# A hand-ordered list of operations replaced by another: sliding attention and a token-mixing MLP on one core

## The chip, the cores and the metric

The kernel runs on one core of one Trainium2 chip. The metric is the device time of one execution in microseconds (us); of several runs the median is given. A profile is one further execution, recorded by the hardware profiler; its span goes from the first to the last instruction that the profiler sees.

A core has five engines that work side by side, each through its own instructions in the order in which they were issued: TensorE (PE in the profile; its weight loads are the row PEld), VectorE (DVE), ScalarE (ACT), GpSimd (POOL) and SyncE (SP), which here only starts DMA transfers. They wait for one another through semaphores. All inputs and outputs are bfloat16.

## The reference

The input `x` is [1, 2048, 512]: 2048 tokens of 512 numbers. Six modulation rows come from a condition `c`. The first part is an attention in which each token looks at itself and at seven earlier tokens, two apart; the second is an MLP that mixes tokens.

```python
mod = (silu(c) @ w_mod).reshape(c.shape[0], 6, 1, -1)
sa, ca, ga, sb, cb, gb = mod[:, 0], ..., mod[:, 5]
h = layernorm(x) * (1 + ca) + sa
# attention: 32 heads of 16; token s attends to s, s-2, ..., s-14
q, k, v = split(h @ wqkv)
logits = einsum('bhsd,bhswd->bhsw', q, k[idx]) * 16 ** -0.5   # masked where idx < 0
o = einsum('bhsw,bhswd->bhsd', softmax(logits), v[idx])
x = x + ga * (o @ wo)
h = layernorm(x) * (1 + cb) + sb
# MLP over tokens: w1 is [2048, 1792], w2 is [1792, 2048]
h = layernorm(h)
u = gelu(einsum('bsd,sf->bdf', h, w1) + b1)
y = einsum('bdf,fs->bds', u, w2) + b2
return x + gb * transpose(y)
```

## The kernel before

**Tiling.** The tokens are 16 tiles of 128. The attention runs over five chunks of 2, 4, 4, 4 and 2 tiles (`SIZES`, chunks 0 to 4). The MLP needs all tokens for each of its 14 output tiles; it is cut into sweeps over the tiles that are ready, and partial sums are parked.

**How the order is made.** The kernel body adds operations to a graph (`_Graph.add`), each with a name, an engine, what it reads and writes, and the buffers that it takes and frees. The text `ORDER` (L182) lists 762 tokens: 760 names and two fillers. `_Graph.schedule` goes through it from front to back and checks that all that an operation depends on stands ahead of it. The loop behind `order = G.schedule()` (L1005) then issues them one by one. Each engine receives its own instructions in the order of this list, and SyncE its DMA starts. So the list decides, for each engine, what stands behind what; a waiting instruction holds up all that stand behind it on its engine, and nothing on the others. A token can carry a mark: `:a`, `:d`, `:p` puts an operation that has a choice on ScalarE, VectorE or GpSimd. `:q` makes `mm()` write each 128-column matmul as four matmuls of 32 columns, each with its own weight load, one behind the other at `tile_position=(0, j)`. `fill:K:N` issues N matmuls of 128x128 on the identity into PSUM buffer `psS[K]`; nobody reads them.

**Buffers.** There are six PSUM buffers `psS` of 512 columns and a double one, `psL`, for logits; a ring of four buffers `big` of 1 MB, and a ring of five, `vd` (tile `vD`). A buffer is given to an operation when the list reaches it: the one freed longest ago in the list. So a new order also gives out other buffers, and the wait for a buffer is a wait for its last reader.

**Recording.** All instructions are issued from one helper (`_EngProxy.wrapped`), so the profile shows L133 for all of them; they are told apart by tiles and shapes.

**Stages and names.** In a name the first number is the chunk, or for single tiles the tile.

- Start: `ident` and `consts` make constants on GpSimd; `ld_c`, `ld_x*`, `ld_wmod*`, `ld_wqkv*` load. `cps`, `silu_exp`, `silu_dve` make silu(c); `modcols1` and `a1col` make the column 1+ca. `wsc{t}_{kt}` multiplies one 128x512 block of the raw Q, K or V weights (t = 0, 1, 2) by it, into `w_qkv`. `ln1s`, `rstd1`, `nb1`, `n1` are the first LayerNorm, `tr` and `hT` (chunks 0, 1) or `xt` (DMA, later chunks) its transpose. `warm` issues nine idle matmuls.
- Attention: `qkv{chunk}_{t}{j}` are the projections and `ev` copies them out of PSUM. `qk{chunk}_{dlo}` multiplies q with the eight shifted k on VectorE, 128x4096 numbers in a chunk of four tiles; `red` sums the products over four of the 16 numbers of a head by matmuls with a 0/1 matrix (`group4`), always as four 32-column tiles. `max`, `sub`, `exp`, `esum`, `rcp`, `smB` are the softmax: VectorE, TensorE, ScalarE, TensorE, ScalarE, VectorE. `a2` and `vd` are DMAs that spread the weights and v over partitions; `halo` copies the 16 tokens ahead of a chunk. `pv` multiplies (VectorE, 128x4096 again), `pvacc` sums (TensorE, four tiles), `oev` copies out.
- Behind it, by tile: `wo` is the output projection, with x added by an identity matmul; `x1` copies it out, `ln2q`, `ln2m`, `rstd2`, `nb2`, `n2` are the second LayerNorm, `aff` the modulation, `ln3s`, `rstd3`, `nb3`, `h3` the third. `modcol`, `mcols`, `mrowt`, `mrows` make the modulation rows, and `st_row`, `ld_row` send them through DRAM to be spread over the partitions as `rows_bc` (0: ga, needed by `woq_s`; 1: sb, 1+cb and gb, needed by `aff`).
- MLP: `mlp1_{sweep}_{ft}_{tile}` are the first layer's matmuls for output tile `ft` from that token tile on; `park` copies partial sums to `gT`, `inj` brings them back, `padd` adds them, `gelu` ends the layer. `mlp2`, `fin` and `st_out` are the second layer, its scaling and the stores.

Of the kernel before, what the change touches and what calls it, by code (L numbers as in the profile page):

```python
# [41 lines left out]
class _Graph:  # L42
# [42 lines left out]
    def schedule(self):  # L85
        by_name = {o.name: o for o in self.ops}
        held = {p: [None] * n for p, n in self.pools.items()}
        freed = {p: [-1] * n for p, n in self.pools.items()}
        done, order = set(), []
        for pos, token in enumerate(ORDER.split()):  # L90
            name, *rest = token.split(":")
            if name == "fill":
                k, n = map(int, rest)
                f = _Op(-1, [("pe", 0.06 * n, lambda k=k, n=n: self.fill_fn(k, n))], 0.0, "filler", 0)
                f.alloc = f.frees = f.behind = None
                order.append(f)
                continue
# [6 lines left out]
            if o.alloc is not None:  # L104
                p = o.alloc.pool
# [82 lines left out]
hT1_3:a qkv0_00 sab ev0_12:d n1_6 ld_wmod4 qvb0 ln1s14 ld_wo1 qkv0_02 qvb_cp0 ln1s15 ev0_00:a wsc2_2 qvb1  # L188
wsc2_0:d qkv1_00 wsc2_3 ev0_10:a ev0_02:d ln1s10 wsc2_1:d qkv1_10 qvb_cp1 qk0_0 ev1_10:a qkv0_22 qk0_1 n1_7
qkv0_20 ln1s13 qk0_2 qkv1_02 xt6 red0_0 ev1_00:a qk0_3 red0_1 red0_2 ev0_22:a ld_wmod5 qkv1_22 qk1_0 ev0_20:a  # L190
qkv1_12 ev1_02:a vd0_1 red0_3 ev1_12:a mask qkv1_11 vd0_0 ln1s11 max0 xt8 qk1_2 qkv1_01 ev1_11:a sub0 qkv1_03
ev1_01:a xt9 exp0 qkv1_13 qk1_1 ev1_03:a xt7 esum0 ev1_13:a qkv1_20 rcp0 vd0_2 ln1s12 qkv1_21 smB0 qk1_3 a2_0_3
# [25 lines left out]
nb2_12 ln2m11 n2_12 mlp1_0_7_4 a2_4_1 ln2m10 h3_8 rstd2_10 ld_w2_4 aff12 mlp1_0_9_4 rstd2_13 rstd2_11 nb2_10
ln3s12 mlp1_0_9_8 mlp1_0_7_8 n2_10 mlp1_0_8_8 nb2_13 pv4_0 park0_7:a mlp1_0_12_4 ld_w1_0_1664 park0_8:a
mlp1_0_11_4 nb2_11 pv4_2 n2_13 mlp1_0_10_4 rstd3_12 pv4_1 park0_9:a mlp1_0_12_8 n2_11 mlp1_0_10_8 pv4_3 inj1_4  # L220
mlp1_0_11_8 ld_w1_1_0 park0_10:a pvacc4_2 ld_w1_1_640 park0_11:a pvacc4_0 nb3_12 aff11 pvacc4_1 h3_12 pvacc4_3
mlp1_0_13_0 aff10 oev4_0:a oev4_2:a aff13 mlp1_0_13_4 ln3s10 wo15 ld_w2_5 ln3s13 rstd3_10 mlp1_0_13_8 wo14 x1_15
# [5 lines left out]
padd1_7 gelu7 mlp1_1_10_10 park1_6:a mlp1_2_2_11 ld_w1_2_640 padd1_10 mlp1_2_2_14 mlp1_2_0_11 padd2_2
mlp1_2_0_14 ld_w2_7 gelu2 mlp1_2_1_11 padd2_0 mlp1_2_1_14 gelu0 mlp1_1_12_10 padd2_1 gelu10 padd1_8 gelu1
mlp1_2_5_11 gelu8 mlp1_2_5_14 gelu9 mlp1_2_6_11 mlp1_2_3_11 padd2_6 mlp1_2_3_14 ld_w2_9 mlp1_2_4_11 padd2_3  # L230
mlp1_2_4_14 padd1_12 gelu3 mlp1_1_13_10 padd2_4 gelu6 padd2_5 gelu4 mlp1_1_11_10 padd1_13 gelu5 gelu13 mlp2_0_0
padd1_11 gelu12 gelu11 mlp2_0_0b ld_w2_11 mlp2_0_0c fin0_0 mlp2_8_0 ld_w2_15 mlp2_4_0 st_out0_0 ld_w2_2 mlp2_9_0
# [806 lines left out]
```

## Time and profile before

| | before |
|---|---|
| device time, median of 3 runs | 207.07 us (206.38 to 207.98) |
| span of the profiled execution | 204.6 us (2.5 us below the median of the runs) |
| mean granted TensorE clock | 0.998 |
| instructions | 4223 |
| ScalarE busy | 120.6 us (59%), 283 instructions |
| GpSimd busy | 13.0 us (6%), 36 instructions |
| DMA | 35.93 MB, 55111 packets, mean 176 GB/s |
| costliest TensorE group, `psS<-h,wst` (first MLP layer) | 254 matmuls, 50.7 us |
| costliest VectorE groups, `big<-a2sb,vD` and `big<-q_sb,k_f` | 20 each, 36.9 and 36.3 us |

Of the profiled execution only the span is listed, no device time of its own; so its 204.6 us stand against the median of the runs. Busy time of TensorE is recorded from the start of a matmul to its modelled end, and neighbours overlap, so a mean of 379 ns in a group says nothing about its pace; the distance from one start to the next does. A busy share of 95% therefore doesn't exclude short stops.

### The profile page before, as it was taken

The numbers are of one execution on the slowest core, as the hardware profiler recorded it, in microseconds if no ns is written. First come the engines' busy times: TensorE is split into PE (matmuls) and PEld (weight loads), VectorE is DVE, ScalarE is ACT, GpSimd is POOL, SyncE is SP. The second block draws the span as 40 slices with busy tenths as digits, with TensorE's granted clock in tenths as the row PEclk, the third lists the DMA queues.
The fourth block names the chain that finished last, engine by engine and source line by source line (L and its number), as shares of the span: only waits on it lengthen the run. The fifth ranks groups of instructions, "written<-read, shape, count | busy, mean of one in ns | idle before, by whom it ended". The sixth has DMA issues, their size and how long they took to land.

```text
span 204.6 us, 4223 instructions
## 1 busy us (share of the span) xinstructions
PE 194.7 (95%) x1655; PEld 103.5 (51%) x1655; DVE 163.3 (80%) x260; ACT 120.6 (59%) x283; POOL 13.0 (6%) x36
## 2 busy tenths in 40 slices
PE   3999999999999997989899999999999999999994
PEld 3988554454455553554344445444444444444453
DVE  2899999999999999999999999975473204369365
ACT  2398998994666899989898876683762000000000
POOL 4122001100000001240000000100000000000000
PEclk9999999999999999999999999999999999999999
DMA  5999494646958976194975179946990930121121
GB/s 141 330 380 348 117 239 107 161 98 201 247 186 267 308 234 251 25 272 110 289 200 115 26 157 263 288 131 200 340 304 3 232 88 16 39 77 51 51 82 51
DMA packets 55111, 35.93 MB, mean 176 GB/s; under 512 B 24628, under 2 KB 52404, under 8 KB 55092
## 3 DMA queue, kind: packets, MB, share of 16 engines
q1 hardware_dynamic: 55084, 35.67, 61.4%
q8 instruction: 13, 0.21, 0.4%
q14 instruction: 6, 0.05, 0.1%
q10 hardware_dynamic: 8, 0.00, 0.0%
HBM read 22.55 MB, written 2.10 MB: 121 GB/s over the span
## 4 chain that ended last, share of the span: by engine, by line
PE 65%; DVE 20%; issue 5%; DMA 5%; SPq 3%; ACT 2%; DVEq 0%
PE psS L133 62%; DVE big L133 9%; DVE h L133 3%; PE psL L133 3%; SPq L133 3%; DVE st L133 3%; DMA wst<-in_B_w_dram 2%; DMA xx<-in_A_x_dram 2%; ACT h L133 1%; DVE mv L133 1%; DVE m L133 1%; DVE lsb L133 1%; DVE ls L133 0%; DVE nb L133 0%; DVE woq L133 0%
## 5 line engine op out<-in xcount | busy, mean ns | idle before, releaser
L133 PE MATMUL psS<-h,wst 128*128 128x512 bf16 (+1 forms) x254 | 50.7, 379 | 1.2 <-POOL h L133 0.7
L133 PE MATMUL psS<-hT,w_qkv 128*128 128x512 bf16 (+3 forms) x312 | 46.2, 339 | 0.3 <-ACT w_qkv L133 0.3
L133 PEld LDWEIGHTS <-wst 128*128 128x128 bf16 (+1 forms) x356 | 28.7, 98 | 32.2 <-issue 3.2
L133 PEld LDWEIGHTS <-w_qkv 128*128 128x128 bf16 (+1 forms) x354 | 29.5, 111 | 21.3 <-issue 3.2
L133 DVE TENSOR_TENSOR big<-a2sb,vD 128x4096 bf16<-128x4096 bf16 (+1 forms) x20 | 36.9, 1876 | 0.0
L133 DVE TENSOR_TENSOR big<-q_sb,k_f 128x4096 bf16<-128x4096 bf16 (+1 forms) x20 | 36.3, 1857 | 0.0
L133 DVE SCALAR_TENSOR_TENSOR h<-psS,bcol,rows_bc 128x512 f32<-128x512 f32 (+2 forms) x18 | 12.4, 690 | 24.4 <-PE psS L133 24.2
L133 PE MATMUL psS<-gT,big 128*128 128x512 bf16 x112 | 24.8, 379 | 0.0
L133 PEld LDWEIGHTS <-big 128*128 128x128 bf16 x144 | 12.0, 97 | 13.2
L133 PEld LDWEIGHTS <-ident 128*128 128x128 bf16 (+1 forms) x203 | 13.9, 111 | 5.9 <-issue 2.8
L133 PE MATMUL psS<-woq,o_sb 128*32 128x512 bf16 (+1 forms) x172 | 16.6, 380 | 0.0
L133 ACT ACTIVATE h<-xx,nb,rs 128x512 bf16<-128x512 bf16 x19 | 15.0, 807 | 0.8 <-DVE nb L133 0.7
L133 DVE TENSOR_TENSOR psS<-psS,gT 128x512 f32<-128x512 f32 x14 | 9.3, 696 | 7.0 <-PE psS L133 7.0
L133 ACT ACTIVATE junk<-xx 128x512 bf16<-128x512 bf16 x22 | 13.8, 626 | 0.2
L133 POOL TENSOR_SCALAR h<-xx,rs,nb 128x512 bf16<-128x512 bf16 x9 | 7.3, 813 | 101.3 <-DVE nb L133 84.0
L133 ACT ACTIVATE lv<-mv,epscol 128x1 f32<-128x1 f32 (+2 forms) x25 | 7.3, 291 | 9.3 <-DVE mv L133 8.4
L133 DVE BATCH_NORM_STATS2 st<-xx 128x6 f32<-128x512 bf16 x14 | 9.5, 678 | 4.0 <-DMA xx<-in_A_x_dram 4.0
L133 ACT ACTIVATE gT<-psS,bcol 128x512 bf16<-128x512 f32 x14 | 8.7, 688 | 6.4 <-DVE psS L133 6.4
L133 PEld LDWEIGHTS <-group 128*32 128x32 bf16 x288 | 6.8, 96 | 10.2 <-issue 4.8
L133 DVE TENSOR_TENSOR h<-h,rows_bc 128x512 bf16<-128x512 bf16 (+2 forms) x20 | 11.5, 581 | 0.5
L133 DVE TENSOR_TENSOR h<-h,xx 128x512 bf16<-128x512 f32 (+2 forms) x18 | 11.4, 633 | 0.6
L133 ACT ACTIVATE gT<-psS 128x512 bf16<-128x512 f32 x19 | 10.8, 587 | 1.6 <-PE psS L133 1.5
(94 smaller groups left out, 220.4 us busy)
## 6 DMA issues: line engine op xcount, KB each, us to landing
vD<-v_sb SPq DMA_DIRECT2D x12, 524.5 KB, 3.8
big<-in_B_w_dram SPq DMA_DIRECT2D x4, 896.0 KB, 8.2
vD<-v_sb SPq DMA_DIRECT2D x8, 268.5 KB, 3.0
wst<-in_B_w_dram SPq DMA_DIRECT2D x3, 640.0 KB, 5.3
out_dram<-h SPq DMA_DIRECT2D x15, 128.0 KB, 1.8
xx<-in_A_x_dram SPq DMA_DIRECT2D x7, 256.0 KB, 6.1
wst<-in_B_w_dram SPq DMA_DIRECT2D x2, 800.0 KB, 4.8
gT<-in_w_mod_dram SPq DMA_DIRECT2D x3, 512.0 KB, 6.1
```

What stands on the lines that cost most here:

```text
L133: r = fn(*a, **k)
```

## The change

Both kernels hold the same 760 operations: the same graph, the same buffers, the same transfers. Changed are the list `ORDER` and the way a filler gets its PSUM buffer: with `fill:N` it takes the buffer that was freed longest ago and is not held, as any other operation does.

- Fillers: 52 and 24 idle matmuls in place of 70 and 16. The first now stands ahead of all LayerNorm work, the second behind `tr0_0` and ahead of `modcols1`.
- `:q` stands at 29 groups in place of 19 (the list before has 19 such tokens), at other groups for the most part; `esum3` is among them. The number of matmuls goes from 1655 to 1753.
- Other engine: `wsc1_2`, `wsc1_1`, `wsc0_1`, `wsc2_0`, `wsc2_1`, `park1_5` from VectorE to ScalarE; `wsc1_0`, `hT0_0`, `hT0_3`, `park1_2`, `park1_4` from ScalarE to VectorE; `halo_v1`, `halo_v3` from ScalarE to GpSimd and `halo_k3` back.
- All else is order: the diff shows the start, the stretch from chunk 2's products to chunk 3's softmax and the first MLP groups, and the places of `h3_6` and `h3_14`.

```diff
@@ -90,7 +90,8 @@
         for pos, token in enumerate(ORDER.split()):
             name, *rest = token.split(":")
             if name == "fill":
-                k, n = map(int, rest)
+                n = int(rest[0])
+                k = min((freed["ps"][i], i) for i in range(self.pools["ps"]) if held["ps"][i] is None)[1]
                 f = _Op(-1, [("pe", 0.06 * n, lambda k=k, n=n: self.fill_fn(k, n))], 0.0, "filler", 0)
                 f.alloc = f.frees = f.behind = None
                 order.append(f)
...
 ORDER = """
-consts ld_x_1_2 act_table ld_x0 ld_x_1_4 ld_c ld_x_2_8 ld_x1 ident ld_x_2_6 ld_wmod1 ln1s3 halo0 ld_wqkv1 cps
-ln1s2 warm2 ld_wqkv0 silu_exp ld_wmod0 ln1s0 ln1s4 ln1s1 ln1s5 rstd1_0 ld_x_4_14 nb1_0 ln1s9 rstd1_1 n1_0 n1_1
-silu_dve nb1_1 ld_wqkv2 ln1s8 fill:2:70 tr0_0 n1_2 n1_4 modcols1 ln1s7 hT0_3:a n1_5 n1_3 ld_x_3_10 hT0_2:d a1col
-hT0_0:a fill:4:16 tr1_2 wsc1_2:d ld_b1 hT0_1:a wsc1_3:d wsc1_0:a tr1_0 wsc1_1:d ln1s6 hT1_2:a ld_wmod2 qkv0_10
-ld_x_3_12 wsc0_0:d rstd1_2 wsc0_1:d qkv0_12 wsc0_2:d hT1_1:a nb1_2 n1_8 n1_9 wsc0_3:d modcols0 hT1_0:d ld_wmod3
...
-ev2_13:a esum1 ev1_23:a qkv2_21 rcp1 vd1_2 red2_0 smB1 ev2_21:a ld_b2 red2_1 qk2_3 halo_v2:a a2_1_1 red2_2
-pvacc0_1 a2_1_3 qkv3_00 a2_1_2 qkv3_10 a2_1_0 pv0_2 mrowt0 vd1_1 qkv2_20 ev3_10:a pv0_3 ev3_00:a red2_3 mrows0:a
...
-ld_w1_0_0 oev1_3:a mrowt1 qkv3_03 mrows1:a x1_0 st_row1 qkv4_00 ev3_03:a vd2_0 ln2q1 qk3_2 pvacc1_0 ev4_02:a
-red3_1 pvacc1_1 oev1_0:a qkv3_23:q oev1_1:a qk3_3 ev4_00:a wo3:q ln2q0 wo5:q pv2_2 qkv4_22:q x1_5 ev3_23:a wo2:q
-ld_row1 ln2q5 ld_w1_0_896 ln2m0 halo_v3:a wo4:q x1_3 pv2_1 x1_2 red3_2 x1_4 red3_3 ln2q3 qkv3_21:q pv2_3 rstd2_0
-qkv4_20 ln2q2 ev3_21:a ev4_22:a vd3_3 pvacc2_1 nb2_0 max3 pvacc2_2 n2_0 warm0 ln2q4 vd3_0 n2_1 ln2m2 sub3 pv2_0
-pvacc2_3 oev2_2:a exp3 rstd2_2 esum3 oev2_1:a aff0 pvacc2_0 rcp3 oev2_0:a qkv4_10 oev2_3:a ln2m4 nb2_2 smB3
...
-ev4_20:a a2_3_3 nb2_4 nb3_0 ln3s3 n2_5 n2_4 vd3_2 warm1 ln3s2 h3_1 h3_0 qkv4_12 aff4 rstd3_2 wo8 x1_7 ld_w2_0
-nb3_2 ln3s5 h3_3 h3_2 ln2q6 ln3s4 mlp1_0_6_0 ev4_12:a pv3_0 mlp1_0_3_0 x1_9 rstd3_4 mlp1_0_5_0 x1_8 mlp1_0_0_0
...
-mlp1_0_10_0 smB4 rstd3_6 ln2m12 a2_4_2 mlp1_0_9_0 h3_7 rstd2_12 h3_6 a2_4_3 ln2q11 h3_9 mlp1_0_8_4 ln2m13 a2_4_0
...
-mlp1_1_5_10 mlp1_1_1_10 inj1_2 ld_w1_2_0 mlp1_1_2_6 h3_11 rstd3_14 park1_1:a h3_14 mlp1_1_4_10 mlp1_1_3_10
...
+ident consts ld_x_1_2 ld_c ld_x0 act_table cps silu_exp silu_dve fill:52 ln1s3 ln1s2 ld_x1 ln1s0 ld_x_1_4 ln1s1 warm2
+ln1s4 ld_x_2_6 rstd1_0 nb1_0 n1_1 ln1s5 rstd1_1 halo0 ln1s7 n1_0 tr0_0 nb1_1 n1_3 hT0_1:a fill:24 ld_wmod1 ld_x_2_8
+ln1s9 modcols1 ld_wqkv1 ld_wqkv0 n1_5 ln1s8 a1col ld_wmod0 hT0_3:d n1_2 n1_4 wsc1_3:d hT0_0:d wsc1_2:a hT0_2:d
+wsc1_1:a tr1_2 hT1_2:a wsc1_0:d ln1s6 tr1_0 hT1_0:d wsc0_0:d ld_x_4_14 rstd1_2 ld_wqkv2 wsc2_3 wsc2_2 ld_wmod3
+wsc0_3:d wsc0_1:a ld_b1 wsc0_2:d nb1_2 n1_8 qkv0_10 hT1_3:a qkv0_12 ev0_12:d qkv0_02 ld_x_3_10 ld_wo3 modcols0
+ev0_10:a ln1s15 qkv0_00 sab qvb0 ln1s14 n1_7 qvb_cp0 hT1_1:a qkv1_10 ev0_02:d qk0_2 n1_6 qvb1 qvb_cp1 n1_9 ld_wmod5
+ev0_00:a ld_x_3_12 qk0_0 wsc2_0:a wsc2_1:a qk0_3 ld_wo0 ln1s11 ev1_10:a qkv1_00 ev1_00:a ld_wmod2 qkv1_02 ev1_02:a
...
+ev3_00:a ev2_22:a halo_v2:a qk2_3 qkv3_10 qkv3_02 a2_1_3 qkv3_01 ev3_01:a qkv2_21 red2_1 red2_2 red2_3 pv1_0 ld_row0
...
+rstd2_0 qk3_2 vd2_2 qkv4_22 x1_4 a2_2_1 red3_1 red3_2 ld_w1_0_512 x1_2 ld_b2 mrowt1 mrows1:a a2_2_3 a2_2_2 vd2_3
+a2_2_0 pv2_0 qkv3_23 ln2q2 pv2_2 red3_3 ln2q4 nb2_0 ld_w1_0_0 max3 qkv4_20 qkv3_21:q ln2m4 wo3:q n2_0 vd2_1 pv2_1
+ev4_22:a pv2_3 ld_w1_0_896 st_row1 ld_row1 sub3 ev3_21:a pvacc2_1 ev3_23:a halo_v4:a ev4_20:a vd4_0 ld_w2_4 vd3_3 x1_3
+ln2q3 pvacc2_2 ln2m2 rstd2_4 n2_1 aff0 exp3 warm3 oev2_2:a rstd2_2 nb2_2 pvacc2_0 oev2_0:a warm1 esum3:q n2_3 pvacc2_3
+oev2_3:a oev2_1:a qkv4_00 vd3_1 vd3_0 rcp3 nb2_4 ln3s1 ln3s0 rstd3_0 n2_2 aff2 warm0 vd4_3 smB3 a2_3_1 a2_3_2 a2_3_0
+qkv4_10 qkv4_12 n2_4 n2_5 ev4_10:a wo6 ev4_00:a x1_6 ln3s2 ln3s3 aff4 wo8:q ev4_12:a rstd3_2 nb3_2 h3_2 x1_8 h3_3
+wo9:q nb3_0 h3_1 h3_0 wo7:q x1_9 ln2q9 mlp1_0_1_0 ln3s4 ln3s5 a2_3_3 mlp1_0_3_0 pv3_0 mlp1_0_0_0:q rstd3_4 nb3_4 x1_7
...
+vd4_1 rstd2_12 h3_6 nb2_12 ln2q13 h3_9 n2_12 mlp1_0_8_0 mlp1_0_8_4 mlp1_0_7_4 h3_8 mlp1_0_7_8 mlp1_0_8_8 ln2m11 a2_4_2
...
+aff14 rstd3_15 nb3_15 h3_15 ln3s14 ld_w1_1_896 rstd3_14 inj1_4 h3_11 inj1_3 mlp1_1_3_6 mlp1_1_3_10 h3_14 mlp1_1_4_6
...
 """
```

More of the change, by code (lines that the diff above doesn't have):

```diff
@@ L188 @@
[L188 to L192, printed above, removed]
@@ L208 @@
-warm3 n2_2 ev4_10:a ln3s0 wo6 a2_3_0 n2_3 ln3s1 a2_3_1 rstd2_4 wo7 x1_6 vd3_1 aff2 rstd3_0 a2_3_2 biascols wo9:q
-ev4_20:a a2_3_3 nb2_4 nb3_0 ln3s3 n2_5 n2_4 vd3_2 warm1 ln3s2 h3_1 h3_0 qkv4_12 aff4 rstd3_2 wo8 x1_7 ld_w2_0
-nb3_2 ln3s5 h3_3 h3_2 ln2q6 ln3s4 mlp1_0_6_0 ev4_12:a pv3_0 mlp1_0_3_0 x1_9 rstd3_4 mlp1_0_5_0 x1_8 mlp1_0_0_0
-biascols_cp:a ln2q8 nb3_4 pv3_1 halo_v4:a mlp1_0_2_0 h3_4 vd4_1 h3_5 mlp1_0_1_0 ln2q9 pv3_2 ld_w2_1 mlp1_0_2_4
-vd4_2 ln2q7 mlp1_0_0_4 vd4_0 mlp1_0_3_4 park0_0:a mlp1_0_1_4 mlp1_0_5_4:q park0_1:a ln2m6 vd4_3 pv3_3 park0_2:a
@@ L218 @@
[L218 to L222, printed above, removed]
@@ L228 @@
[L228 to L232, printed above, removed]
@@ new lines @@
+aff14 rstd3_15 nb3_15 h3_15 ln3s14 ld_w1_1_896 rstd3_14 inj1_4 h3_11 inj1_3 mlp1_1_3_6 mlp1_1_3_10 h3_14 mlp1_1_4_6
+mlp1_1_4_10 park1_1:a park1_2:d park1_3:d park1_4:d mlp1_1_8_10 mlp1_1_9_10 padd1_8 gelu8 park1_5:a ld_w1_2_0
+mlp1_2_0_11 mlp1_2_4_11 mlp1_2_4_14 padd2_4 ld_w2_5 gelu4 park1_6:a mlp1_1_10_10 padd1_10 mlp1_1_7_10 padd1_7 gelu7
+mlp1_2_2_11 mlp1_2_2_14 padd2_2 mlp1_2_0_14 gelu10 ld_w1_1_1408 mlp1_2_3_11 mlp1_2_1_11 mlp1_2_1_14 ld_w1_2_640
+padd2_0 padd2_1 gelu1 mlp1_1_11_10 gelu0 mlp1_2_3_14 padd2_3 mlp1_2_5_11 mlp1_2_6_11 mlp1_2_5_14 gelu3 padd2_6 gelu6
@@ L238 @@
+fin15_0 st_out14_0 mlp2_15_1 fin15_1 st_out15_0 mlp2_15_2 st_out15_1 fin15_2 st_out15_2
 """
```

51 lines of the change are left out of this document (30 added, 21 removed).

## The prediction

> **What bounds the kernel now.** I read the busy shares first, then busy time by stretches, then the waits, then the timelines of TensorE, VectorE and ScalarE.
>
> The first two parts of the page and the stretches (columns: length, then TensorE, weight loads, VectorE, ScalarE and GpSimd busy, with instructions):
>
> ```profile
> PE 194.7 (95%) x1655; PEld 103.5 (51%) x1655; DVE 163.3 (80%) x260; ACT 120.6 (59%) x283; POOL 13.0 (6%) x36
> ...
> DVE  2899999999999999999999999975473204369365
> ```
>
> ```profile
> 13.61:57.00 43.39, 43.39 (x395) 24.68 (x396) 43.10 (x52) 36.09 (x78) 3.41 (x5) 1.00 0.73 200
> 57.00:92.00 35.00, 32.69 (x448) 18.36 (x446) 34.42 (x44) 29.68 (x78) 4.22 (x5) 1.00 0.70 217
> 92.00:113.00 21.00, 19.75 (x218) 8.82 (x217) 20.72 (x24) 19.36 (x50) 0.00 (x0) 1.00 0.70 175
> ```
>
> TensorE is never free for long, but from 7 to 136 us VectorE is just as full, and ScalarE is at 83 to 92%. So TensorE sets the end, and VectorE sets where TensorE has to stop. The chain of waits says the same: TensorE from 13.61 to 57, mostly VectorE from 57 to 112, TensorE from 112.83 to 201.58. The places where TensorE stood still carry a bracket in its timeline:
>
> ```profile
> 13.61 1.94 PE L133 MATMUL psS<-hT,w_qkv 128*128 128x256 bf16 x16 [0.26 <-ACT w_qkv L133]
> ...
> 79.71 0.59 PE L133 MATMUL psL<-m,nident 128*128 128x512 bf16 x2 [0.74 <-DVE m L133]
> ...
> 81.41 0.61 PE L133 MATMUL psS<-lsb,ident 128*128 128x128 bf16 x8 [0.57 <-ACT lsb L133]
> ...
> 91.52 7.18 PE L133 MATMUL psS<-h,wst 128*128 128x512 bf16 x38 [0.68 <-POOL h L133]
> ...
> 101.61 0.61 PE L133 MATMUL psS<-big,group 128*32 128x512 bf16 x8 [0.73 <-DVE big L133]
> ```
>
> A sum makes this exact. Start to start, a 512-wide matmul takes 0.216 us, a 256-wide one 0.109, a 128-wide one 0.056. I add these in program order from the first projection (13.61), with the mode switches below. The work is 182.7 us, so an unstopped TensorE would finish at 196.3. Its last group really ends at 201.4: 5.1 us are waits. The same sum over VectorE from chunk 1's first logit product (24.02) puts `h3_6` at 113.4; it really ended 1.2 us later, and TensorE's `mlp1_0_8_4`, which needs it, started at 114.56 as soon as it was there. **The limit is VectorE up to h3_6 plus 86.8 us of matmuls behind it.** Those 86.8 us hold the same matmuls in the new list.
>
> **TensorE work: more.** 19 groups carry the four-tile mark in the old list, 29 in the new. Such a group costs what the whole one costs:
>
> ```profile
> 60.71 1.04 PE L133 MATMUL psS<-woq,o_sb 128*128 128x512 bf16 x4
> 61.59 0.38 PE L133 MATMUL psS<-xx,ident 128*128 128x512 bf16 x1
> 61.90 1.06 PE L133 MATMUL psS<-hT,w_qkv 128*32 128x512 bf16 x16
> 62.89 1.04 PE L133 MATMUL psS<-woq,o_sb 128*128 128x512 bf16 x4
> ...
> 70.37 1.04 PE L133 MATMUL psS<-woq,o_sb 128*32 128x512 bf16 x16
> 71.24 0.39 PE L133 MATMUL psS<-xx,ident 128*32 128x512 bf16 x4
> ```
>
> Sixteen quarter matmuls take 71.24 - 70.37 = 0.87 us, four whole ones 0.88. What costs is the passage. The identity matmul before the four-tile group at 61.90 takes 0.31 us instead of 0.216 (0.09 more), and the group takes 0.99 instead of 0.87 until the whole one at 62.89 starts (0.12 to 0.13 more). A pair costs 0.23 us. In program order I count 34 passages before and 46 after: 12 x 0.114 = +1.4 us. That is the opposite of what more four-tile groups suggest: they now stand in shorter runs. One group has no row: `esum3`, eight 128-wide matmuls in quarters. Below, it costs nothing more (quarters as above); above, 0.109 us each as a 256-wide one in quarters, so +0.4. I take nothing: TensorE waits behind it for h3 anyway, and ScalarE, which reads it, is late there. The Trainium skill ("TensorE: Matmul & The Clock Gate", LDWEIGHTS) gives a weight load columns/1.2 GHz, and "TensorEngine Tiling (Array Packing)", Restrictions, says that column tiling loses the fast weight load: four loads of 32 columns would be 107 ns against 56, +0.4 us at `esum3` alone; for 512-wide groups they hide, as the 0.87 us shows.
>
> New work from the first projection: 182.7 + 1.4 = 184.1 us.
>
> **The start: earlier.** These are my terms:
>
> - SyncE's queue issues tile 1 of x third instead of fifth. Tile 0 landed 2.6 us after its issue, so tile 1 should land near 4.8 instead of 7.30. VectorE's statistics then run dense from 3.65 (0.39 us of idle at 7.33 goes), tile 1's are done at 6.9 instead of 8.24, and `tr0_0` waits for TensorE, not for x.
> - `ident` goes ahead of `consts` on GpSimd (1.7 us before it), `ld_c` ahead of the table load. TensorE starts near 2.4 (c_t lands at 2.25) instead of 3.09. `silu_dve` now heads VectorE's queue, with all statistics behind it; it should end by 3.5, before x lands at 3.62.
> - Idle matmuls: 52 + 9 (`warm2`) from 2.4 at 0.107 us end at 8.95; `tr0_0` to 9.4; 24 more at 0.056 to 10.75; `modcols1` to 11.2. Before, `modcols1` stood ahead of its second filler.
> - `a1col` follows `ln1s8` on VectorE: the x tiles 8 and 9 land at 9.8 (the same bytes ahead as `ld_wmod1` had), two statistics of 0.82, so 11.5 instead of 12.17.
> - Weight scaling: the raw K weights land at 11.26 as before. VectorE does `wsc1_3`, three hT copies and `wsc1_0`, to 12.6; ScalarE does `wsc1_2` and `wsc1_1` at 0.62 each (row: 0.72 with overlap), 11.55 to 12.85. First projection at 12.95 instead of 13.61: **-0.65 us**.
>
> Five scalings move to ScalarE and three short pieces to VectorE, a net -0.65 us for VectorE and about +1.9 for ScalarE in its fullest stretch. Adding ScalarE's queue (dense from 11.55: 10.9 us of rows) gives `ev1_00` at 22.6. VectorE, which waits there, begins chunk 1's products at 22.85 instead of 24.02.
>
> **The middle: fewer waits.** I carried three sums side by side, each instruction at its row's duration, and at each meeting took the latest.
>
> - VectorE reaches `qk2_3` with all of `pv0` done, at 49.35; before it ended at 48.4 with 2.3 us of `pv0` open. It ends `max3` at 76.0 (79.66) and `smB3` at 86.1, with `ln3s0`, `ln3s1` and `aff2` already done, which took before until 87.4. A lead of 1.2 to 1.5 us persists.
> - `sub3` no longer waits (0.74 before): TensorE comes at 77.1, `max3` is 1 us older. Next late is `pv2_1` (78.5): 0.9 us. `esum3` waits for `exp3`, ScalarE at 81.45: 0.3 us.
> - `mlp1_0_1_0` needs `h3_0`, last of 10.4 us dense ScalarE work from 80.5: 90.9. TensorE comes at 90.3: 0.65 us.
> - The `pv3` products end at 100.05 (101.56), `h3_6` at 113.05 (114.67). TensorE comes to `mlp1_0_8_4` at 113.5: no wait.
>
> TensorE's waits add up to 3.3 us instead of 5.1.
>
> SyncE: `st_row1` moves from 66.32 to about 73.1, because `mrowt1` now stands behind `red3_2`. Behind it stand `ld_row1`, `vd4_0`, `ld_w2_4` and `vd3_3`. The first row transfer took 2.6 us from store to load, the second 5.9 under weight loads; a load lands 3.3 us after issue. `aff0` needs it at 81.0: there at 79.0 with 2.6, at 82.3 with 5.9. I take 2.6, since the weight loads are over by then. The w1 loads keep 5 us or more from release to use, against 5 us of landing.
>
> After 113.5 the last LayerNorm chain gives `h3_14` at 134.6 against TensorE's 135.3: free by 0.7 us. PSUM hand-overs in the GELU stretch are free by 0.25 us at the tightest (`gelu1` before `mlp1_2_5_11`).
>
> **Sum.** 12.95 + 184.1 + 3.3 = 200.35 against 201.4: -1.1 us. The tail is unchanged. Span 204.6 - 1.1 = 203.5. The median of the runs, 207.07, lies 2.5 us above the profiled span; I keep that: **206.0 us**, -0.5%.
>
> **Rivals.**
>
> 1. The early lead is lost. If the idle matmuls stay slow, the 24 take 2.6 us instead of 1.35, `a1col` comes 1.1 us later, and start and VectorE follow: 206.0 + 1.1 = 207.1. For it: in the trace of before the spacing went from 0.107 to 0.056 only at 9.0 us, 6 us after the first matmul. Against: TensorE now starts 0.7 us earlier. The Trainium skill ("TensorE: Matmul & The Clock Gate", Part 1) has a free-running window of 3.4 us after which the clock doubles, so the doubling may come anywhere from 5.8 to 9.2 us here; the 6 us of the trace agree.
> 2. Slower: ScalarE becomes the bound. It frees nearly every PSUM slot, and the new list leaves it 10 us without a gap before `h3_0`. `mlp1_0_1_0` already waits for it, so whatever ScalarE is later there goes whole into the end. The nearest price is the moved work, 1.9 us, if none of it falls into gaps, and 1.3 us more if `aff0` also waits for `ld_row1` (82.3): 206.0 + 3.2 = 209.2. It decides from 1.1 us of lateness, where the gain is used up, and passes 1% at 3.1 us. Against: ScalarE has 7 us of idle time between 13.6 and 57.
> 3. The passages cost nothing where TensorE waits anyway, the 1.4 us vanish into the 3.3, and VectorE's lead of 1.6 is all: 207.07 - 1.6 - 0.65 = 204.8. That needs `h3_0` earlier than I put it.
> 4. The new list does nothing that counts: 207.1, the same as the first.
>
> **Numbers.** Forecast (205 to 206.8) 0.38; lead lost or nothing 0.18; ScalarE bound 0.26, of it 0.22 beyond 1%; better than 205 0.18. One per cent, 2.1 us, is about what a measurement of this kernel can tell. So faster by over 1% (below 205.0) has 0.18, slower by over 1% (above 209.1) 0.22, within it 0.60. The range goes from 203.7, where half of the cases better than 205 remain, to 209.6, where half of the ScalarE cases beyond 1% do: 2 in 10 are left out.
>
> **What would show it.** First projection at 12.95; idle spacing halved before 9.4; first 4096-wide product at 22.85; no bracket at `sub3`; a wait of about 0.9 us before the `pv2_1` reduction; `h3_6` ending near 113; TensorE dense from 113.5 to 200.4. Wrong if ScalarE rows show late PSUM reads between 20 and 50 us, if `aff0` waits for rows_bc, or if waits of TensorE sum to over 5 us.

## The result and the profile after

Of 20 runs each, the new kernel takes 207.67 us (206.50 to 210.49) and the one before 206.93 us (206.05 to 207.98). The ratio is 1.0039, with an interval from 1.0021 to 1.0058: **0.8 us slower**, within the one per cent, where I had forecast 0.5% faster (206.0 us). As a ratio I had given 206.0/207.07 = 0.9948; the miss is 0.91%, 1.9 us, and the sign was wrong. A few runs show a mean granted TensorE clock of 0.992 and took 208.55 to 210.49 us: two of these 20 of the new kernel, five of the twelve of the run with fewer passages below, at most one in any other run, and none of the 89 of the kernel before in the series below.

The page after, its first two parts (span; busy time; VectorE's slices):

```profile
span 205.4 us, 4408 instructions
...
PE 194.4 (95%) x1753; PEld 101.5 (49%) x1753; DVE 163.6 (80%) x259; ACT 122.3 (60%) x283; POOL 16.2 (8%) x37
...
DVE  3898999998999999999999999984565500577565
```

Nothing stands out: the same shares, 98 matmuls more. The stretches from the first projection on (length; TensorE, weight loads, VectorE, ScalarE, GpSimd busy):

```profile
12.78:57.00 44.22, 42.47 (x458) 24.35 (x459) 42.54 (x49) 36.29 (x80) 4.91 (x5) 1.00 0.72 199
57.00:92.00 35.00, 33.25 (x460) 17.93 (x458) 34.45 (x44) 30.36 (x79) 5.10 (x5) 1.00 0.75 229
```

The first projection comes at 12.78 instead of 13.61, but in the stretch behind it VectorE is idle for 44.22 - 42.54 = 1.7 us, where it was 0.3 us before. The timeline of VectorE shows three of these stops, with what ended them in the bracket, and two slow products:

```profile
16.14 0.69 DVE L134 BATCH_NORM_STATS2 st<-xx 128x6 f32<-128x512 bf16 x1 [0.39 <-DMA xx<-in_A_x_dram]
...
20.14 2.77 DVE L134 TENSOR_TENSOR big<-q_sb,k_f 128x2048 bf16<-128x2048 bf16 x2
...
35.08 0.21 DVE L134 SCALAR_TENSOR_TENSOR nb<-mv,rs 128x4 f32<-128x4 f32 x1 [0.28 <-ACT rs L134]
...
43.84 2.28 DVE L134 TENSOR_TENSOR big<-q_sb,k_f 128x4096 bf16<-128x4096 bf16 x1
46.79 4.49 DVE L134 TENSOR_TENSOR big<-q_sb,k_f 128x4096 bf16<-128x4096 bf16 x2 [0.67 <-ACT k_f L134]
```

`ln1s15` waits 0.39 us for tile 15 of x. The two products from 20.14 (`qk0_0`, `qk0_3`) take 2.77 us, where such a product took 1.22 before; `qk0_0` alone takes 1.64, and GpSimd scales V weights beside it. `nb1_3` waits 0.28 us for `rstd1_3` on ScalarE. And `qk2_2` waits 0.67 us for something that ScalarE writes to `k_f`. In the kernel before, the same products (four of `qk0`, then `qk1_0`; the line gives the first one's shape) ran without a stop:

```profile
19.48 6.82 DVE L133 TENSOR_TENSOR big<-q_sb,k_f 128x2048 bf16<-128x2048 bf16 x5
```

The timeline of TensorE, at the places that I had shown of before:

```profile
12.78 1.21 PE L134 MATMUL psS<-hT,w_qkv 128*128 128x256 bf16 x8 [0.56 <-DVE w_qkv L134]
...
78.52 0.61 PE L134 MATMUL psL<-m,nident 128*128 128x512 bf16 x2
80.55 1.05 PE L134 MATMUL psS<-big,group 128*32 128x512 bf16 x16 [1.43 <-DVE big L134]
...
92.71 3.73 PE L134 MATMUL psS<-h,wst 128*128 128x512 bf16 x40 [0.68 <-ACT h L134]
...
99.40 0.61 PE L134 MATMUL psS<-big,group 128*32 128x512 bf16 x8
```

`sub3` (78.52) has no bracket any more, as forecast. The stop moved to `pvacc2_1` behind it (80.55), and the one ahead of the MLP (92.71) is as long as before. From 99.40 on TensorE is dense until 202.4.

The chain of waits changed its middle. By engine, it now says

```profile
PE 64%; ACT 10%; DVE 10%; DMA 6%; SPq 5%; issue 3%; DVEq 0%; ACTq 0%
```

where ScalarE had 2% and VectorE 20% of it: from 77.6 to 98.9 us it runs through ScalarE, which has no gap there of more than 0.3 us.

### The profile page after: what moved, and what is told of

Its sections match the earlier page's. It is cut to its first block, busy times and chain, and to the rows that moved or that the text cites. A ratio compares the mean times of both kernels' runs of the same rounds, so it can differ in the third digit from the quotient of the medians.

```text
span 205.4 us, 4408 instructions
## 1 busy us (share of the span) xinstructions
PE 194.4 (95%) x1753; PEld 101.5 (49%) x1753; DVE 163.6 (80%) x259; ACT 122.3 (60%) x283; POOL 16.2 (8%) x37
## 4 chain that ended last, share of the span: by engine, by line
PE 64%; ACT 10%; DVE 10%; DMA 6%; SPq 5%; issue 3%; DVEq 0%; ACTq 0%
PE psS L134 62%; DVE big L134 8%; SPq L134 5%; DMA xx<-in_A_x_dram 4%; ACT h L134 2%; DMA a2sb<-lsb 2%; PE psL L134 2%; ACT junk L134 2%; ACT xx L134 1%; ACT o_sb L134 1%; ACT v_sb L134 1%; DVE woq L134 1%; DVE lsb L134 0%; ACT lv L134 0%; ACT k_f L134 0%
## 5 line engine op out<-in xcount | busy, mean ns | idle before, releaser
L134 PE MATMUL psS<-hT,w_qkv 128*32 128x512 bf16 (+2 forms) x372 | 46.8, 354 | 0.6 <-DVE w_qkv L134 0.6
L134 DVE TENSOR_TENSOR big<-q_sb,k_f 128x4096 bf16<-128x4096 bf16 (+1 forms) x20 | 37.0, 1881 | 0.8 <-ACT k_f L134 0.7
L134 PEld LDWEIGHTS <-ident 128*128 128x128 bf16 (+1 forms) x214 | 12.3, 107 | 4.8 <-issue 2.1
L134 ACT ACTIVATE v_sb<-psS,qvb 128x512 bf16<-128x512 f32 (+1 forms) x20 | 11.2, 594 | 3.2 <-PE psS L134 3.2
L134 DVE TENSOR_TENSOR h<-h,rows_bc 128x512 bf16<-128x512 bf16 (+2 forms) x20 | 11.5, 579 | 0.3
L134 ACT ACTIVATE q_sb<-psS,qvb 128x512 bf16<-128x512 f32 (+1 forms) x18 | 10.5, 609 | 1.9 <-PE psS L134 1.9
```

The costliest lines, as they stand in the source:

```text
L134: r = fn(*a, **k)
```

## The experiments

In the diffs a line stands for a stretch of the list. "Stops" of VectorE below are gaps of more than 0.08 us between two of its operations from 10 to 116 us, added up from the trace. The wait of `ln1s9` for x 8 and 9 falls just outside in the first execution of the new kernel (0.46 us, at 9.85) and in some others. Ratios are to the kernel before in the same series of runs. Each kernel has 6 to 12 timed runs, one of them profiled; the second executions of the kernel before, of the new start and of the kernel with halo and transfers moved are single ones.

**The halo.** `qk2_2` started 0.03 us after `halo_k3` had ended. It reads chunk 2's keys; `halo_k3` writes the 16 columns ahead of chunk 3's keys, elsewhere in the same tile `k_f`. The list's own dependencies have no edge between the two.

```diff
 ev2_13:a
-halo_k3:a
 qkv2_03:q red2_0 qk2_2 a2_1_0 a2_1_2 ev2_03:a a2_1_1 qkv3_00 ev3_00:a ev2_22:a halo_v2:a qk2_3
+halo_k3:a
```

> One token moved in the new list: halo_k3 goes behind qk2_3, so that the product qk2_2 does not have to wait for it. In the new kernel VectorE stood still for 0.67 us until 46.79, just after halo_k3 ended (46.76). My theory: up to h3_6 the time is VectorE's, so the 0.67 us come out at the end: qk2_2 starts at about 46.2, h3_6 ends near 114.6, span 204.8, time 0.6 us under the new kernel, that is +0.1% against the kernel before. Rival A: qk2_2 waited for ev2_13 (ended 46.47) and not for the halo; then only 0.3 us go. Rival B: ScalarE's chain into h3_0 sets the middle; VectorE gains 0.67 at qk2_2 but h3_0 and the end stay, +0.4%. The start is unchanged, so tiles 14 and 15 of x should land near 16.1 and the raw V weights near 18.2 again if these landings are a matter of the order.

Measured: 206.59 us, ratio 1.0003 (0.9979 to 1.0028). VectorE goes from `qk2_1` through `qk2_3` without a stop:

```profile
43.00 6.69 DVE L134 TENSOR_TENSOR big<-q_sb,k_f 128x4096 bf16<-128x4096 bf16 x3
```

So it was the halo and not `ev2_13`: here `qk2_2` started at 45.21, before `ev2_13` had ended (45.53). `qk2_2` started 0.03 us after `halo_k3` had ended in all six profiled executions with the halo ahead of it on ScalarE, with stops of 0.57 to 0.82 us, and in none with the new place. The built programs say the same: in the new kernel `qk2_2` waits for ScalarE's semaphore to reach 74, the count that `halo_k3` sets; with the halo moved it waits for 71, while `ev2_13` sets 73. `halo_k3` writes 16 columns in each of the four parts of the tile; `qk2_2` reads none of them, but its region lies between the first and the last of these pieces. But x's tiles 14 and 15 landed at 15.46 here and not at 16.1, the V weights at 16.95, and `qk0_0` took 1.21 us: these are not a matter of the order alone. And a new stop appears, 1.04 us ahead of `pv3_0`:

```profile
92.19 2.29 DVE L134 TENSOR_TENSOR big<-a2sb,vD 128x4096 bf16<-128x4096 bf16 x1 [1.04 <-DMA a2sb<-lsb]
```

**The loads of the start.** The loads alone, in SyncE's order:

```diff
-ld_x_4_14 ld_wqkv2 ld_wmod3 ld_b1 ld_x_3_10 ld_wo3 ld_wmod5 ld_x_3_12
+ld_x_4_14 ld_wqkv2 ld_x_3_10 ld_b1 ld_x_3_12 ld_wmod5 ld_wo3 ld_wmod3
```

> Only SyncE's queue is changed in the new list: ld_wmod3, ld_wo3 and ld_wmod5 stand behind ld_x_3_12, and ld_b1 behind ld_x_3_10, so behind the raw V weights stand the same loads as in the kernel before. My theory: the loads issued behind them took part of the bandwidth in the new kernel; now x 14 and 15 land near 14.7 and the V weights near 16.5, GpSimd scales its two blocks at 16.6 to 18.0 and is off VectorE's products, qk0_0 takes 1.22 us and not 1.64, the 0.39 us before ln1s15 go, qk1_0 starts at 23.2 (24.11), the end 0.9 us earlier: -0.05% against the kernel before. Rival: the landings spread from one execution to the next or hang on what stands ahead; then x 14 lands at 16.1 again, qk1_0 stays at 24.1 and the time at +0.4%.

Measured: 207.58 us, 1.0030 (1.0004 to 1.0056), no difference that can be told from the new kernel. My theory falls. x 14 and 15 landed at 15.3, V at 17.0, but with both edits together at 16.4 and 17.9. Over the thirteen profiled executions whose loads up to there stand as in the new kernel, x 14 and 15 land between 14.95 and 16.57 and V between 16.4 and 18.7; in two of the kernel before at 14.7 and 15.3, and at 16.4 and 16.9. Most of the spread belongs to the execution.

**Both.**

> Both edits together, the halo's place and the order of the loads. If the two make up what the forecast missed, qk2_3 ends at 49.7 (51.28 in the new kernel, 49.35 forecast), h3_6 at 113.6, and the time is 1.5 us under the new kernel: 206.1, -0.35% against the kernel before. If the gain at the start is lost in ScalarE's chain, it stays within 0.3 us of the new kernel.

Measured: 206.94 us, 0.9994 (0.9971 to 1.0017). Against the loads alone this is the halo's effect a second time: 0.9994 - 1.0030 = -0.36%, as 1.0003 - 1.0039 = -0.36% in the first pair. Each is 0.75 us, with some 0.7 us to either side by the intervals, or about 0.5 for the two together.

**The passages.** Only `:q` marks change: 24 passages instead of 46.

```diff
-qkv1_20:q vd0_2 ln1v10 nb1_4 red1_0
+qkv1_20 vd0_2 ln1v10 nb1_4 red1_0
...
-mlp1_0_1_4 vd3_2 mlp1_0_0_4
+mlp1_0_1_4:q vd3_2 mlp1_0_0_4:q
...
```

> Only the four-tile marks of the new list are changed: 24 passages between whole and four-tile matmuls in place of 46, with 30 marked groups. By the passage of 0.114 us that is 2.5 us less work for TensorE, all of it before h3_6. My theory: VectorE sets the time up to h3_6, so TensorE only waits longer: its waits before mlp1_0_8_4 grow by about 2 us and the time falls by 0.3 us at most, +0.25% against the kernel before. Rival: TensorE's work sets the time; then the time falls by 1.5 to 2.5 us, -0.3 to -0.8%.

Measured: 207.67 us, 1.0036 (1.0007 to 1.0065): the same as the new kernel. In the profiled execution TensorE stops longer, 2.1 us instead of 1.5 at `pvacc2_1` and 0.95 instead of 0.75 at `mlp1_0_1_0`, and it runs into a stop that the new kernel doesn't have:

```profile
110.26 0.20 PE L134 MATMUL psS<-ident,b_t 14*128 14x14 bf16 x2
111.06 2.12 PE L134 MATMUL psS<-h,wst 128*128 128x512 bf16 x9 [0.59 <-DMA wst<-in_B_w_dram]
```

A w1 load (`ld_w1_0_1152`) lands at 111.0 there; in the new kernel TensorE comes to it only after 111.8. So in the profile much of the work saved turns into waits, and the median shows no gain. This isn't settled, though: five of the twelve runs had a granted clock of 0.992, and the other seven have a median of 206.89 us, 0.75 us under the new kernel's 207.64 at full clock. A gain of that size, half of the least that the rival forecast, is not excluded.

**The two halves.** Each half of the new list with the other half of the old.

```diff
 new list up to qkv0_10
-new list behind it
+old list behind it, less what has been issued
```

> The new list up to the first projection (qkv0_10), fillers included, and behind it all other operations in the order and on the engines of the list before: the start alone. In three profiled executions of this start the first projection came at 12.78, 12.47 and 12.41, against 13.61 in the one of the kernel before, whose VectorE has no stop of more than 0.08 us from 10 us on. If the lead of about 1 us is real and VectorE carries it through, the time falls by 0.6 to 1.0 us: -0.3 to -0.5% against the kernel before. Rival: what follows waits for transfers (raw V weights, x) that land no earlier, and the lead is gone by 24 us: within 0.1%.

> The list before up to qkv0_10, and behind it the new list: the rest alone. The whole change measured +0.4%. If the start is worth -0.4%, the rest must be worth +0.8% here (waits of VectorE: 0.67 us at qk2_2, 0.28 at nb1_3, and what ScalarE passes on); if the start is worth nothing, +0.4%. The forecast had put the rest at -0.2%: TensorE's work 1.4 us more, its waits 1.8 us fewer. This run also gives a second execution of the old start: qkv0_10 at 13.6 if it is steady.

Measured: the start alone 207.44 us, 1.0034 (1.0008 to 1.0059); the rest alone 208.42 us, 1.0082 (1.0058 to 1.0106). So ahead of the new rest the new start is worth 1.0039 - 1.0082 = -0.43%, 0.9 us, near the lead that was forecast. The rest is where it is lost: +0.8%, 1.7 us, where I had -0.2%. That the start alone is slower I had expected in neither form. In two profiled executions of it the first projection came at 12.71 and 12.92, against 13.61 and 13.06 in two of the kernel before, and `qk1_0` at 23.77 and 23.74, against 24.02 and 23.97: of a lead of 0.1 to 0.9 us some 0.25 are left, as VectorE waits there for `ev1_00`, which ScalarE ends at 23.7. The old rest's order puts statistics of x ahead of `ev1_00` on ScalarE, and ScalarE stood still for x ahead of them, 0.88 us in the first execution and 0.54 in the second. These two executions took 206.28 us each, two single ones of the kernel before 206.56 and 207.29.

> The new start with the old rest again, for a typical execution: the first profile was one of its fastest (206.28 us against a median of 207.44). Theory: the new start hands VectorE transfers without slack (x 8 and 9, x 14 and 15, raw V weights), so here stops of 0.4 to 1 us appear ahead of ln1s9 or ln1s14/15, or a chunk 0 product takes 1.6 us beside GpSimd, and qk1_0 comes at 24.2 to 24.8. Rival: qk1_0 comes at 23.8 again and the loss is later.

In the second profile `ln1s9` waits 0.63 us for x 8 and 9 (0.25 in the first), but `qk1_0` comes at 23.74 all the same. Why the median of the start alone is 0.9 us above the kernel before stays open; neither profiled execution shows it.

**The transfers ahead of a2_3.**

```diff
 halo_v4:a ev4_20:a
-vd4_0 ld_w2_4
 vd3_3
 ...
 aff2 warm0
-vd4_3
 smB3 a2_3_1 a2_3_2 a2_3_0
 ...
 ln3s4 ln3s5 a2_3_3
+vd4_0 ld_w2_4 vd4_3
```

with the halo's edit.

> The kernel with the halo moved, and on SyncE's queue vd4_0, ld_w2_4 and vd4_3 moved from ahead of the four a2_3 transfers to behind them. In the run with the halo alone VectorE stood still for 1.04 us ahead of pv3_0 until a2_3_3 had landed (issued 89.29, landed 91.97; smB3 ended 86.46), and nb3_4, h3_4 and TensorE (0.8 us at mlp1_0_1_4 and mlp1_0_0_4) waited behind it. My theory: the three transfers ahead (1.5 MB, landing until 87.9) slow the a2 transfers; without them a2_3_3 lands at most 4.2 us after smB3, pv3_0 does not wait, and the time falls by another 0.3 to 0.8 us: -0.2 to -0.3% against the kernel before. Rival: the a2 transfers are slow by themselves (four issues of 0.65 us and 2.1 us to land), then a2_3_3 still comes 5 us after smB3 and the time stays at +0.0%.

Measured: 206.54 us, 0.9996 (0.9969 to 1.0022). The profiled execution agrees with the theory: `a2_3_3` lands at 90.57, 4.2 us after `smB3`, and `pv3_0` follows without a stop.

```profile
91.08 2.29 DVE L134 TENSOR_TENSOR big<-a2sb,vD 128x4096 bf16<-128x4096 bf16 x1
```

It starts 1.1 us earlier than in the run with the halo alone, from the same `qk1_0` (23.06), and the span is 1.1 us shorter (203.7 against 204.8). The timed runs don't show it: 0.9996 against 1.0003, with intervals of 0.25% to either side. A second execution tells why:

> The kernel with the halo and the three transfers moved again, for a typical execution: its first profile (205.85 us, VectorE's stops 0.56 us in all) lay under its median of 206.54. Stops by landings (ln1s9, ln1s15, pv0_3, aff0) should add up to 0.5 to 1 us more here, with qk2_2 and pv3_0 free.

It took 207.11 us with 2.37 us of VectorE's stops in place of 0.56: `ln1s9` 0.90 (x 8 and 9 landed at 10.07 instead of 9.46), `pv0_3` 0.44, `nb1_3` 0.28, `aff0` 0.18, `nb2_2` 0.34, `qk0_2` and `qvb_cp0` 0.23 together. `qk2_2` and `pv3_0` are free.

**The fillers.** `fill:70` and `fill:16` in place of 52 and 24.

> The new list with the old numbers of idle matmuls, 70 and 16 in place of 52 and 24. In the new kernel TensorE stands still for 1.0 us between the first filler with warm2 (end 7.65) and tr0_0 (8.66), which waits for n1_0 on GpSimd; 18 more matmuls at 0.056 us fill just this. The second filler ends 0.45 us earlier, so modcols1 too, but a1col waits for VectorE (ln1s8 until 11.56). So no difference: within 0.1% of the new kernel, +0.4%. Rival: fewer matmuls ahead of modcols1 bring a1col forward, -0.2%; or the clock comes later and the first projections are slower, +0.2%.

Measured: 208.09 us, 1.0057 (1.0031 to 1.0083). Its interval overlaps that of the new kernel; 0.18% more is no difference that these runs can tell, and no gain. Neither rival shows in the profile, where the idle matmuls are fast from 7.20 us on and the first projection starts at 12.32, earlier than in the new kernel; 0.18% is, however, about the size of the second rival, so the timed runs don't exclude it. The idle matmuls' spacing halves (to 0.056 us) anywhere from 3.0 to 6.0 us after the first matmul, in the sixteen profiled executions of all these kernels.

**The stop ahead of the MLP.** With the edits to halo and transfers, `nb3_0` ahead of `aff4` and `h3_0`, `h3_1` ahead of `h3_2`, `h3_3`; in a second kernel also `n2_4` on GpSimd.

```diff
-ln3s2 ln3s3 aff4 wo8:q ev4_12:a rstd3_2 nb3_2 h3_2 x1_8 h3_3 wo9:q nb3_0 h3_1 h3_0
+ln3s2 ln3s3 nb3_0 aff4 wo8:q ev4_12:a rstd3_2 nb3_2 h3_0 h3_1 h3_2 x1_8 h3_3 wo9:q
...
-    NE=('PAPAAPAADAAPAAPD', 'PAPAAPAAAADAAADP', 'APPAAADDDDADAADA'),
+    NE=('PAPAAPAADAAPAAPD', 'PAPAPPAAAADAAADP', 'APPAAADDDDADAADA'),
```

> The kernel with the halo and the three transfers moved, and the third LayerNorm of tiles 0 to 3 in the order in which TensorE uses them: nb3_0 stands ahead of aff4, and h3_0 and h3_1 ahead of h3_2 and h3_3. In the new kernel and in every run so far TensorE stood still for 0.74 us (0.95 in one) ahead of mlp1_0_1_0 until h3_0, the last of the four, was there. Theory that ScalarE's dense stretch from exp3 to h3_0 sets the end: h3_0 comes 0.8 us earlier, the stop at mlp1_0_1_0 goes, those at pvacc3_3 (0.3) stay, and the time falls by 0.4 to 0.7 us against the run without this edit, to -0.3% against the kernel before. Rival, that VectorE still sets it: TensorE only waits later (pvacc3_3, mlp1_0_10_0), less than 0.2 us.

> The same, and n2_4 (0.80 us on ScalarE) on GpSimd, which is idle there: one letter in the table of engines. If ScalarE sets the end, another 0.3 to 0.6 us go, as the stop at pvacc3_3 goes too (its PSUM buffer is freed by oev3_0, the last of ScalarE's dense row); floor: the load ld_w1_0_1152 lands at 109.3 or later, and mlp1_0_10_0 cannot start before. Together -0.5% against the kernel before. Rival: GpSimd slows VectorE beside it (as qk0_0 took 1.64 us in place of 1.22 beside a scaling on GpSimd) and it comes out even or worse.

Measured: 207.54 us, 1.0020 (0.9999 to 1.0041), and 207.97 us, 1.0041 (1.0020 to 1.0061): not faster but slower than without. The stop ahead of `mlp1_0_1_0` is gone in the first and is 0.33 us inside the group in the second, where it waits for `h3_2` on GpSimd; TensorE stops later instead, 0.24 to 0.33 us twice behind 95 us and 0.39 at `pvacc3_3`. VectorE got slower, because GpSimd now runs beside `aff4`, whose inputs are both in SBUF. VectorE, then GpSimd, of the first of the two kernels:

```profile
88.88 1.86 DVE L134 TENSOR_TENSOR h<-h,rows_bc 128x1024 bf16<-128x1024 bf16 x2
```

```profile
89.06 1.14 POOL L134 TENSOR_SCALAR h<-h,rs,nb 128x512 bf16<-128x512 bf16 x1 [3.75 <-DVE nb L134]
```

`aff4` takes 1.86 us in place of 1.40, `h3_1` on GpSimd 1.14 in place of 0.77. In the second kernel `aff2` has the same 1.85 us beside `n2_4`. So these edits don't test the place of ScalarE cleanly: they cost VectorE 0.46 or 0.9 us. In the first of them TensorE starts the group behind `pvacc3_3` at 99.57, exactly where the second execution without these edits has it, though the 0.64 us ahead of `mlp1_0_1_0` are gone: the gain was lost again by then. Whether it would be lost with VectorE at its old pace isn't shown.

**The same kernels again.**

> The new kernel unchanged, a second profiled execution. If the 0.39 us ahead of ln1s15 and the slow qk0_0 (1.64 us) belong to one execution, they are gone or different here: x 14 and 15 land between 15.3 and 16.4, qk1_0 starts between 22.9 and 24.1. The stop at qk2_2 (0.6 to 0.7) and those of TensorE at pvacc2_1 (1.5) and mlp1_0_1_0 (0.75) must be here again, if they belong to the order. Time +0.4% again.

Measured: 207.73 us, 1.0040 (1.0019 to 1.0061). `qk0_0` takes 1.22 us here and x 14 and 15 land at 15.06, but VectorE's stops add up to 2.56 us: `ln1s9` 0.44, `nb1_3` 0.28, `qk2_2` 0.82, `pv3_0` 0.79 and two small ones. TensorE stops 1.46 us at `pvacc2_1` and 0.74 at `mlp1_0_1_0`, as before.

> The kernel before, unchanged, a second profiled execution. In the first, VectorE had no stop of more than 0.08 us from 10 us on, while five executions with the new rest had 1.2 to 2.6 us of them. If that is the order, VectorE's stops from 10 to 116 us stay under 0.4 us here; if the first execution was a lucky one, they are over 1 us.

One execution of the kernel before: 206.56 us, VectorE's stops 0.19 us. x 14 and 15 landed 0.6 us later than in its first execution, the K weights at 11.86 and not 11.26, and nothing came of it. From 23.97 on VectorE is dense, through the place where the new list waits:

```profile
36.19 2.71 DVE L133 TENSOR_TENSOR big<-a2sb,vD 128x2048 bf16<-128x2048 bf16 x2
38.82 6.68 DVE L133 TENSOR_TENSOR big<-q_sb,k_f 128x4096 bf16<-128x4096 bf16 x3
```

## Why the prediction was wrong

What I had forecast, against one profiled execution of each kernel (us):

| | forecast | new kernel | halo moved | halo and transfers | kernel before |
|---|---|---|---|---|---|
| first projection starts | 12.95 | 12.78 | 12.47 | 12.41 | 13.61 |
| `qk1_0` starts | 22.85 | 24.11 | 23.06 | 23.06 | 24.02 |
| `qk2_3` ends | 49.35 | 51.28 | 49.69 | 49.58 | 48.44 |
| `max3` ends | 76.0 | 77.96 | 76.33 | 76.23 | 79.66 |
| `smB3` ends | 86.1 | 88.11 | 86.46 | 86.37 | 84.45 |
| `h3_0` ends (in the list before, `h3_2` comes last of tiles 0 to 3, at 91.47) | 90.9 | 92.66 | 91.02 | 90.93 | 89.00 |
| `pv3` products end | 100.05 | 102.16 | 101.53 | 100.43 | 101.56 |
| `h3_6` ends | 113.05 | 115.24 | 114.61 | 113.51 | 114.67 |
| span | 203.5 | 205.4 | 204.8 | 203.7 | 204.6 |

The column of the halo and the transfers is the forecast, to 0.6 us at each line: the sum fits an execution whose VectorE hardly stops (0.56 us). That is the better of two executions of this kernel, by luck: the other has a span of 205.1, and the timed runs of this kernel are level with the kernel before (0.9996), not 0.5% faster. **The step that failed is "The middle: fewer waits"**, where VectorE "reaches `qk2_3` with all of `pv0` done, at 49.35". I had carried the sums with waits at the meetings that the list's dependencies and slots name, and found none for VectorE there. In the new kernel it ended at 51.28, 1.93 us later, and that is the sum of its stops and slow products up to there: 0.39 (`ln1s15`), 0.10 (`qk0_2`), 0.28 (`nb1_3`), 0.67 (`qk2_2`) and 0.50 (`qk0_2` and `qk0_0` beside GpSimd), 1.94 in all. All later lines of the new kernel are late by 1.8 to 2.2.

- **A wait that the list doesn't know**: the halo, 0.67 us in this execution. That it costs time is settled by two pairs of timed runs; its size by them, 0.75 us, is good to about 0.5.
- **A wait that the list does name and the sums passed over**: `nb1_3` behind `rstd1_3` on ScalarE, 0.28 us. It and the 0.10 ahead of `qk0_2` stand, at the same size, in all twelve profiled executions of lists with the new rest; the kernel before has 0.09 and nothing there.
- **No room for transfers.** The other 0.89 us are losses that differ from one execution to the next: 0.5 us of GpSimd and 0.39 at `ln1s15` in the first, 0.79 at `pv3_0` in the second. In twelve profiled executions of lists with the new rest, VectorE's stops are 0.6 to 2.7 us (in six of them 0.6 to 0.8 by the halo); in two of the kernel before 0.1 and 0.2. I had checked each transfer for its landing in the one profiled execution and found it in time; the old list took x 14 and 15 0.6 us later without a stop, the new one stops at such shifts. That these stops make up what is left of the miss in the timed runs is inferred from the profiles: the one edit at a stop of this kind (`pv3_0`) moved its profiled execution by 1.1 us and the timed runs by nothing that can be told. So of the 1.9 us the halo's part is shown, and the rest stays in part open.

The other steps:

- *The start*: right in the profile. 12.78 for 12.95, TensorE at 2.24, `a1col` 11.47 for 11.5; in the second execution 13.07 and 3.01. By the timed runs it is worth 0.9 us ahead of the new rest and a loss ahead of the old one, which is not explained. The list issues the load of x 8 and 9 seventh instead of fourth; it landed between 9.2 and 10.4 us in the thirteen executions with the new start, and the first projection started 2.9 to 3.2 us behind it in each. I had taken 9.8, which is their middle, but given it no spread. `qk1_0` was at fault too: 22.85 was forecast, and the eleven executions with the new start and the new rest have 22.89 to 24.58, 23.5 in the mean. I had put it at its earliest.
- *TensorE's work*: right. 46 passages in the trace, and from 12.78 to the end 184.3 us and the stops, for 184.1. That the passages hardly matter where TensorE waits anyway is likely from the profile without 22 of them, but open in its timed runs. `esum3` in quarters has 0.46 us to the next group, eight times 0.056 as if whole. The extra 0.4 us, my estimate from the loss of the fast weight load that the Trainium skill ("TensorEngine Tiling (Array Packing)", Restrictions) states for column tiling, is not there.
- *The waits* (from start to start, so a little more than the brackets): `sub3` free, as forecast; `pvacc2_1` 1.49 us for 0.9, `mlp1_0_1_0` 0.75 for 0.65. Not forecast: `wo1` 0.92 (behind `woq_s` on VectorE), `red1_3` 0.62, `pvacc1_3` 0.39, `pvacc3_3`, `qvb0` and `esum1` 0.3 each. Together 5.2 us for 3.3, over the 5 us that the prediction had named as a sign of being wrong. The start was 0.2 us earlier and the work 0.2 us more than forecast, so the waits are the whole difference at the end.
- *The rows*: about right in this execution. `st_row1` was issued at 74.49 (forecast 73.1), `ld_row1` 3.0 us behind it at 77.47, for the 2.6 that I chose, and it landed 3.5 us later, at 80.96. VectorE was late itself (`aff0` at 83.01), so it cost nothing. In other executions the load stood up to 4.9 us behind the store, and `aff0` waited for it: 0.34 us in the run with `n2_4` on GpSimd, 0.31 with halo and loads moved.
- *Tail and GELU stretch*: right. `h3_14` ended 0.6 us before TensorE started the group that reads it, and TensorE has no stop after 99.4.
- *From span to time*: too much by 0.5 us. I had added 2.5 us; in the runs that list both, the time is 2.0 us above the span. By this measure the profiled execution of the kernel before was 0.5 us faster than the median. The term raised the forecast time, so it doesn't explain the miss, and it falls out of the ratio.

The rivals: the lead was not lost by the clock (first fast idle matmul at 6.36, and at 8.95 in the second execution, both ahead of the 9.4 that the prediction named). ScalarE is indeed dense from 77.6 to 98.9 us, and the chain of waits runs through it. But it does not make the new kernel late by itself: in the run with the halo moved `h3_0` came 1.6 us earlier with the same ScalarE work, as VectorE was 1.05 us earlier at `qk1_0` and had no stop of 0.67 at `qk2_2`. Whether less work on ScalarE there would shorten the time is not shown. The slower end came by neither of the prices that I gave for it.

GpSimd beside VectorE I had not priced at all. In the first execution V's weights landed at 18.23, so that their scaling on GpSimd (from 18.39 on) fell on the chunk 0 products:

```profile
18.39 2.32 POOL L134 TENSOR_SCALAR w_qkv<-h,a1col 128x512 bf16<-128x512 bf16 x2 [7.38 <-DMA h<-in_A_wqkv_dram]
```

The product takes 1.64 us for 1.22, and the second scaling 1.65 for the first one's 0.69. The Trainium skill ("SBUF — State Buffer", Who interferes with whom) says that a VectorE instruction with two SBUF inputs contends with a GpSimd instruction that reads SBUF, and that the lock on the ports that they share is exclusive. The trace agrees, and it fits that they take turns: `wsc2_2` on GpSimd is there at 19.06 but ends at 20.71, about its 0.69 us after the next instruction behind `qk0_2` started on VectorE (20.07); `qk0_0`, there from 20.14, loses 0.42 us meanwhile.

## What to carry to other kernels

A list of dependencies is not the list of waits. Here a small write into a tile that a large product reads held the product, though the two share no column; that the tool goes by the span from the first to the last column written is inferred. Look for such waits in the built program, or for writes to the same tile between two instructions of the engine that bounds, in the order that is to be tried.

An order whose sum keeps the bounding engine dense may do so with no margin. Compare the same transfer's landing in several executions, and give each transfer that the bounding engine waits for at least that spread. Here, as far as the profiles show, an order with a better sum and less room lost to one with room. One profiled execution per kernel can be a microsecond off its median here (203.7 and 205.1 us of span for one kernel), so a term under that size needs timed runs, in pairs.

## What I had not expected of the hardware

- Landings of the same load, in the same order, spread over 1.6 us (x 14 and 15: 14.95 to 16.57, issued between 6.5 and 7.8) and 2.3 us (V weights: 16.4 to 18.7), and not in the order of the issue times: one issued at 6.97 landed at 16.12, one at 7.79 at 15.32. By 14 us the new kernel's first execution had moved as much as that of the one before (3.96 and 3.89 MB), yet x 14 and 15, with the same bytes ahead of them in the queue, landed 1.4 us later; in the second executions they landed 0.3 us earlier.
- A VectorE instruction with two inputs in SBUF and a GpSimd operation that reads SBUF, side by side, made each other longer: 1.64 instead of 1.22 us and 1.65 instead of 0.69, 1.86 instead of 1.40 and 1.14 instead of 0.77.
- Matmuls of 128 columns in quarters cost the same as whole ones: eight took 0.46 us to the next group, 0.056 each.
